# A pre-LayerNorm transformer block whose LayerNorm steps on VectorE change their form, with the planner's constants that go with them

## The chip, the cores and the metric

The kernel runs on one core of a Trainium2 chip. A core has five engines that run side by side [...]: TensorE (PE, matrix products), ScalarE (ACT, functions such as the exponential), VectorE (DVE), GpSimd (POOL), and SyncE (SP), which here issues nearly all DMAs. The metric is the device time of one execution in microseconds, the median of several runs.

## What is computed

One transformer block on 2048 rows of 640 in bf16: attention with 32 heads of 20 that share one key and one value head, then a gated MLP with 1536 hidden units, each behind a LayerNorm without weights and with a residual.

```python
def _layernorm(x, axis=-1, eps=1e-5):
    m = jnp.mean(x, axis=axis, keepdims=True)
    v = jnp.var(x, axis=axis, keepdims=True)
    return (x - m) / jnp.sqrt(v + eps)
...
q = (x @ wq).reshape(B, S, H, Dh).transpose(0, 2, 1, 3)
k = x @ wk
v = x @ wv
scores = jnp.einsum("bhqd,bkd->bhqk", q, k) * (Dh ** -0.5)
p = _softmax(scores, axis=-1)
o = jnp.einsum("bhqk,bkd->bhqd", p, v)      # heads joined, then @ wo
...
g = jnp.einsum("bsd,df->bsf", x, w_gate)
u = jnp.einsum("bsd,df->bsf", x, w_up)
return jnp.einsum("bsf,fd->bsd", _gelu(g) * u, w_down)
...
h = x + _A_ref(_layernorm(x), A_wq, A_wk, A_wv, A_wo)
h2 = h + _B_ref(_layernorm(h), B_w_gate, B_w_up, B_w_down)
```

## The kernel before

**Tiles and stages.** The rows are 16 tiles of 128. LN1 normalises each tile, and the result is transposed (tiles 0 and 1 on TensorE, the others by a DMA transpose) into xn1T. From it come the keys kT4, the values v_ext and the queries. The queries are worked in nine chunks of 2, 2, 2, 2, 2, 2, 2, 1 and 1 tiles, and a chunk is split into units of 512 columns, 32 units in all. For each unit and each of the 16 key tiles one *pack* of four score blocks (128 keys x 512 columns, one PSUM bank each) is computed; that is 512 packs and 2048 blocks. When a unit's weighted sums are complete, they are copied to osb, transposed by DMA to onr, divided by the softmax sum into onq (normed, L681), and when a chunk is complete its onq tiles are transposed by DMA to onT (L762), multiplied by wo and added to x. Then LN2 follows on those tiles, their DMA transpose to xn2T, and the MLP of the chunk, which runs beside the attention of the next chunk. The last tile's MLP comes alone at the end.

**Two ways to an exponential.** ScalarE takes blocks one or two at a time (L1519). VectorE can take a block too (L1620): it writes a 16-bit integer to pd slot 0 whose bits, read as bf16, approximate the exponential. Two shifted copies of it in pd slots 1 and 2 refine it; they come from integer adds, usually both in one GpSimd instruction (add_both, L1586), or one of the two on VectorE (do_adds, L1562) and the other alone on GpSimd (L1568). All three copies enter the weighted sum, so such a block costs TensorE three products in place of one. There are eight pd slots.

**The order.** Nothing is decided on the chip. When the program is built, a planner (_Plan) simulates the five engines with a fixed cost and a latency for each operation, and at each moment a greedy rule for an engine picks what it issues next (pe_decide, act_decide, dve_decide, pool_decide, sp_decide). The lists that result are emitted with semaphore waits, and each engine executes its list strictly in order. A cost that is changed therefore changes the whole order after it, and an operation that takes longer than planned stalls its engine's list.

Rules that matter here:
- issue_qk (L1120) decides how many of a pack's four blocks VectorE takes. One is usual. Two are taken when VectorE's expected load (dve_load, L1085) is under 450 ns, few adds are pending, and the comparison of ScalarE's expected stalls leaves more than SP2G (L1135, below). In dve_load each pending half add counts ADDW/2 and each block that waits ADDW on top of its 600.
- dve_decide (L1596) considers an add on VectorE only when at least PADD_LEN adds are pending.
- The norm of a tile (L513) is a task with lock set (L509): dve_decide holds it back while GpSimd's list reaches more than LOCKW = 200 ns ahead (L1653), commit (L80) places it after the GpSimd operation that runs at its start and GpSimd's next operation after it, and pool_decide (L1687) issues nothing while such a norm is due within YIELD = 500 ns. The VectorE adds are committed with lock as well.
- A DMA transpose costs SP 1330 ns and is taken as visible 1700 ns later for LN1 and LN2, 1500 ns later for onr and onT.

```python
            stall(t, 1, fb) + 1382.0 - stall(t, 2, fb) - 956.0 > SP2G[ph]):
```

**LayerNorm.** ln_half (L434) makes bn_stats of each half row and bn_aggr, giving mean and variance in mv. ln_group (L446) then takes the one or two tiles of a group together: the variances are copied to bf16 (L455, ln_vb), EPS is added (L459, ln_veb), GpSimd takes the square root as a power of 0.5 (L463, ln_denb), and VectorE the reciprocal (L467, ln_r). Then each tile is normalised by one tensor_scalar with two per-partition scalars (L513). LN1 has nine groups at the start, LN2 nine over the run.

Of the kernel before, what the change touches and what calls it, by code (L numbers as in the profile page):

```python
# [4 lines left out]
ALU = mybir.AluOpType  # L5
BF16 = mybir.dt.bfloat16
# [3 lines left out]
P = 128  # L10
# [7 lines left out]
CH_W = (1.0, 0.79296875, 0.63671875)  # L18
# [201 lines left out]
def bass_sequential_preLN__grouped_kv_mqa__glu_gated_geglu__prompt_kernel(  # L220
# [87 lines left out]
    xn_tmp = sb("xn_tmp", [P, NXT, D], BF16)  # L308
    stats = sb("stats", [P, 2, NT, 12], F32)
    mv = sb("mv", [P, 2, NT, 2], F32)  # L310
    ln_vb = sb("ln_vb", [P, 2, NT], BF16)
    ln_veb = sb("ln_veb", [P, 2, NT], BF16)
    ln_denb = sb("ln_denb", [P, 2, NT], BF16)
    ln_r = sb("ln_r", [P, 2, NT], F32)
    wq_stage = gbuf[:].rearrange("p f n -> p (f n)")[:, 0:NC_D * D].rearrange("p (c n) -> p c n", c=NC_D)
    pd16 = pd[:].bitcast(BF16)
# [34 lines left out]
    SP2 = 1  # L351
    SP2D = (450.0, 450.0, 450.0)
    SP2P = (3, 3, 3)
    SP2G = (300.0, 300.0, 300.0)
    ADD_MIN = 1
    PVF = 99
    QUIET = 0.55
    FTODO = 4
    PADD_DVE = 1
    PADD_LEN = (3, 3, 3)  # L360
    PRA = 3
    PRD = 3
    TH0 = 1500.0
# [8 lines left out]
    YIELD = 500.0  # L372
    WQA = 1
    W_LAT = 3000.0
    ADDW = 100.0
    MISCMAX = 1500.0
    L_PE, L_ACT, L_DVE, L_POOL = 232.0, 310.0, 150.0, 100.0

# [1 line left out]
    def load(eng, o, i, key, lat, after=()):  # L380
        return plan.commit(eng, (lambda e: e.dma_start(o, i)), 480.0, lat, reads=after, writes=key, dma=True)

    load("sp", xh[:, 0, :], x_view[:, 0, :], [("x", 0)], 2000)
    load("act", wk_sb[:], cview(A_wk), ["wk"], 2500)
    load("sp", xh[:, 1, :], x_view[:, 1, :], [("x", 1)], 2300)
    load("act", wq_stage[:, :, 0:HALF], cview(A_wq)[:, :, 0:HALF], [("wqs", 0)], 4500)
# [9 lines left out]
    def pool(fn, cost, reads=(), writes=()):  # L396
# [4 lines left out]
    pool(lambda e: e.affine_select(out=ident[:], in_=ident[:], compare_op=ALU.not_equal, fill=1.0, base=0,  # L401
                                   pattern=[[-1, P]], channel_multiplier=1), 450, ["ident0"], ["ident"])
    pool(lambda e: e.memset(halfc[:], 0.5), 40, writes=["halfc"])
    pool(lambda e: e.memset(wk4[:].bitcast(F32), 0.0), 300, writes=["wk4z"])
    pool(lambda e: e.memset(wq_pad[:, 0:4, :, :].bitcast(F32), 0.0), 1150, writes=[("wqz", 0)])
    plan.commit("dve", lambda e: e.memset(wq_pad[:, 4:8, :, :].bitcast(F32), 0.0), 1400, L_DVE,
# [39 lines left out]
    def ln_group(ln, tiles, prio, done):  # L446
        n = len(tiles)
        sl = slice(tiles[0], tiles[-1] + 1)
        cnt = [0]
        kk = (ln, tiles[0])  # L450

        def after_stats(op):
            cnt[0] += 1
            if cnt[0] == n:
                dve(lambda e: e.tensor_copy(ln_vb[:, ln, sl], mv[:, ln, sl, 1]), 80,  # L455
                    [("mv", ln, t) for t in tiles], [("vb", kk)], prio, c2)

        def c2(op):
            dve(lambda e: e.tensor_scalar_add(ln_veb[:, ln, sl], ln_vb[:, ln, sl], EPS), 80,  # L459
                [("vb", kk)], [("veb", kk)], prio, c3)  # L460

        def c3(op):
            task(("pool",), lambda e: e.tensor_tensor(ln_denb[:, ln, sl], ln_veb[:, ln, sl], halfc[:, 0:n], ALU.pow),  # L463
                 780, L_POOL, [("veb", kk), "halfc"], [("den", kk)], prio, c4)

        def c4(op):
            dve(lambda e: e.reciprocal(ln_r[:, ln, sl], ln_denb[:, ln, sl]), 90, [("den", kk)], [("lr", kk)],  # L467
                prio, c5)

        def c5(op):  # L470
            for t in tiles:
                norm(t)

        def norm(t):
            slot = []

            def gate():
                return bool(slots["xt"])

            def start():  # L480
                slot.append(slots["xt"].pop(0))
                return slot[0]

            def then(op):
                s = slot[0]

                def tdone(op2):
                    slots["xt"].append(s)
                    done(t, op2)

                if ln == 0:
                    o = xn1T[:, :, t * P:(t + 1) * P]
                    wkeys = [("xn1T", t)]
                else:
                    o = xn2T[:, :, xcol[t]:xcol[t] + P]
                    wkeys = [("xn2T", xcol[t])]
                def free():
                    return ln == 0 or all(up_left[x] == 0 for x in xshare[batch_of[t]])

                if t in (PE_T1 if ln == 0 else PE_T2):  # L500
                    tr_job(("tr", ln, t), xn_tmp[:, s, :], ("xt", s), o, wkeys, lambda: slots["xt"].append(s),
                           lambda op2: done(t, op2))
                    return
                sp_tasks.append(_Task(("sp",), lambda e: e.dma_start_transpose(o, xn_tmp[:, s, :]), 1330, 1700,
                                      [("xt", s)], wkeys, prio, tdone, free))

            keys = [("x", t)] if ln == 0 else [("h", t, 0), ("h", t, 1)]
            tk = _Task(("dve",), None, 320, L_DVE, keys + [("lr", kk)], [], prio, then, gate)
            tk.lock = True  # L509

            def bind():
                s = start()
                tk.fn = lambda e: e.tensor_scalar(xn_tmp[:, s, :], xh[:, t, :], mv[:, ln, t, 0:1],  # L513
                                                  ln_r[:, ln, t:t + 1], ALU.subtract, ALU.mult)
                tk.writes = [("xt", s)]

            tk.born = bind
            tasks.append(tk)

        return after_stats  # L520
# [68 lines left out]
    def kv_job(tiles):  # L589
        n = len(tiles) * P  # L590
        t0 = tiles[0]
        pieces = []
        for c in range(NC_D):
            pieces.append((mm(lambda b: bank(b, n), wk4[:, c, :], xn1T[:, c, t0 * P:t0 * P + n],
                              c == 0, c == NC_D - 1), c_mm(n), [("xn1T", t) for t in tiles] + ["wk4k", "wk4v"]))

        def then(b):
            def kfin(op):
                for t in tiles:
                    key_ready[t] = op  # L600
# [12 lines left out]

        def vthen(b):
            nt = len(tiles)
            vi = ps[:, b * 512:b * 512 + 32 * nt].rearrange("p (t e) -> p t e", t=nt)[:, :, 0:Dh]

            def vfin(op):
                free_bank(b)
                for w in (1, 2):  # L620
                    task(("pool",), (lambda w: lambda e: e.tensor_scalar(
                        v_ext[:, t0:t0 + nt, w, 0:Dh], v_ext[:, t0:t0 + nt, 0, 0:Dh], CH_W[w], None, ALU.mult))(w),
                        180 + 75 * nt, L_POOL, [("v", t, 0) for t in tiles] + [("vone", w)],
                        [("v", t, w) for t in tiles], 0)
# [96 lines left out]
    def on_job(u, so):  # L721
        if u["id"] in PE_ON:
            pieces = []
            for j in range(4):
                pieces.append((mm((lambda j: lambda b: ps[:, b * 512 + j * P:b * 512 + (j + 1) * P])(j),
                                  osb[:, so, j * P:(j + 1) * P], ident[:], True, True), c_mm(128),
                               [("osb", so), "ident"]))

            def then(b):
                slots["osb"].append(so)  # L730
                normed(u, so, bank(b), ("b", b), lambda: free_bank(b))
            jobs.append(_Job(("on", u["id"]), 1.5, pieces, then,
                             lambda: all(x in on_sent for t in u["tiles"] for x in on_before[t])))
            return
        tk = _Task(("sp",), None, 1330, 1500, [("osb", so)], [], 0.5, None, lambda: bool(slots["onr"]))
        sl = []

        def bind():
            s = slots["onr"].pop(0)
            sl.append(s)  # L740
            tk.writes = [("onr", s)]
            tk.fn = lambda e: e.dma_start_transpose(onr[:, s, :].rearrange("p (j i) -> p j i", j=4), osb[:, so, :])

        def sent(op):
            s = sl[0]
# [15 lines left out]

    def on_transpose(t):  # L762
        sl = []
        tk = _Task(("sp",), None, 1330, 1500, [("onq", onslot[t], g) for g in range(NG)], [], 1.0, None,
                   lambda: bool(slots["onT"]))

        def bind():
# [1071 lines left out]
```

The softmax here doesn't subtract the row's maximum and nothing guards it: scores larger than these inputs give would overflow.

## Time and profile before

| quantity | us |
|---|---|
| median of 6 runs (lowest to highest) | 787.71 (786.75 to 790.07) |
| the profiled execution's own time | 789.03 |
| its span, first to last instruction | 787.2 |
| ScalarE exponentials, 413 of two blocks and 598 of one | 437.8 + 363.3 |
| VectorE exponentials, 624 | 417.5 |
| GpSimd double adds, 577 | 588.1 |
| GpSimd single adds, 47 | 31.5 |
| VectorE adds, 25 | 15.4 |

In the profile, busy is the time in which an engine has at least one instruction under way; the sum of the durations of a group can be more, since two neighbours on one engine overlap. The mean duration of a group includes what an instruction waits after it has started. "Idle before" is the time in which the engine had nothing and what released it. The lines of a helper stand for every operation that it issues, so L565 is every piece of projection or MLP on TensorE. The last attention pack's exponentials end at 760.9 us; what follows is the last tile's output projection, LN2 and MLP, one after the other.

### The profile page before, as it was taken

How to read it: one execution, taken by the hardware profiler on the slowest of the kernel's cores; microseconds unless marked ns; L12 is line 12 of the kernel's file. 1: busy time of each engine (PE TensorE's matmuls, PEld its weight loads, DVE VectorE, ACT ScalarE, POOL GpSimd, SP SyncE). 2: the span in 40 equal slices, each digit the busy share in tenths (PEclk: the TensorE clock that was granted, in tenths of full speed). 3: DMA queues.
4: the chain of work that ended last, by engine and by line, in shares of the span. 5: the costliest groups of instructions: out<-in, count | busy, mean ns of one | idle time of the engine just before them, and what ended most of it. 6: DMA issues, size and time to landing. Idle time of an engine off the chain costs nothing.

```text
span 787.2 us, 29885 instructions
## 1 busy us (share of the span) xinstructions
PE 702.0 (89%) x13140; PEld 332.9 (42%) x13140; DVE 610.5 (78%) x1096; ACT 730.1 (93%) x1058; POOL 660.9 (84%) x713
## 2 busy tenths in 40 slices
PE   4698888888889998999888899899998999989998
PEld 3332233432335454444234444445543444434467
DVE  7768878778888777877787777777779787878854
ACT  5799999999999998999999999999999999999981
POOL 5489998989989898888998989789888898889760
PEclk9999999999999999999999999999999999999999
DMA  6554401000110002100010002200021000111000
GB/s 195 85 126 139 119 8 25 19 10 8 25 26 9 2 26 27 26 26 8 9 26 19 9 10 43 26 26 3 10 42 26 9 2 18 35 25 18 11 20 18
DMA packets 56769, 25.90 MB, mean 33 GB/s; under 512 B 47808, under 2 KB 55360, under 8 KB 56640
## 3 DMA queue, kind: packets, MB, share of 16 engines
q1 hardware_dynamic: 55328, 23.55, 13.9%
q8 instruction: 105, 1.72, 1.0%
q10 hardware_dynamic: 1312, 0.44, 0.2%
q14 instruction: 24, 0.20, 0.1%
HBM read 10.21 MB, written 2.62 MB: 16 GB/s over the span
## 4 chain that ended last, share of the span: by engine, by line
PE 53%; ACT 23%; DVE 17%; DMA 4%; issue 2%; POOL 1%
PE ps L565 20%; ACT pa L1519 19%; PE ps L1256 15%; PE ps L1177 15%; DVE pd L1620 9%; PE ps L561 3%; ACT gbuf L905 3%; DVE xn_tmp L513 1%; DVE osb L1283 1%; DMA onT<-onq 1%; DMA onr<-osb 1%; DVE stats L443 1%; PE ps L1382 1%; DMA xh<-in_A_x_dram 1%; ACT L1519 1%
## 5 line engine op out<-in xcount | busy, mean ns | idle before, releaser
L1519 ACT ACTIVATE pa<-ps 128x512 bf16<-128x512 f32 (+1 forms) x1011 | 684.6, 814 | 27.8 <-PE ps L1177 22.6
L1586 POOL TENSOR_TENSOR pd<-pd,shifts 128x512 int32<-128x512 int32 x577 | 588.1, 1039 | 75.8 <-DVE pd L1620 70.8
L1620 DVE TENSOR_SCALAR pd<-ps 128x512 uint16<-128x512 f32 x624 | 417.5, 687 | 139.6 <-PE ps L1177 131.0
L1256 PE MATMUL ps<-pd,v_ext 128*32 128x512 bf16 x1872 | 285.3, 384 | 18.3 <-DVE osb L1283 11.9
L1256 PE MATMUL ps<-pa,v_ext 128*32 128x512 bf16 x1424 | 256.8, 384 | 4.4 <-ACT pa L1519 2.0
L1177 PE MATMUL ps<-qT,kT 32*128 32x512 bf16 x2048 | 203.0, 385 | 40.7 <-DVE pd L1620 22.9
L1177 PEld LDWEIGHTS ps<-qT,kT 32*128 32x128 bf16 x2048 | 56.1, 91 | 205.7 <-DVE pd L1620 127.2
L1256 PEld LDWEIGHTS ps<-pd,v_ext 128*32 128x32 bf16 x1872 | 78.1, 95 | 79.1 <-issue 32.3
L1256 PEld LDWEIGHTS ps<-pa,v_ext 128*32 128x32 bf16 x1424 | 69.9, 95 | 42.9 <-issue 22.3
L565 PE MATMUL ps<-xn2T,wg_sb 128*32 128x256 bf16 (+1 forms) x1736 | 68.0, 272 | 1.4 <-DMA xn2T<-xn_tmp 0.7
L565 PE MATMUL ps<-xn2T,wu_sb 128*32 128x256 bf16 x1680 | 67.2, 274 | 1.9 <-DVE gbuf L922 1.5
L565 PE MATMUL ps<-wd_sb,gbuf 128*32 128x320 bf16 x1344 | 66.3, 301 | 0.0
L565 PE MATMUL ps<-xn1T,wq_pad 128*32 128x256 bf16 (+1 forms) x1440 | 51.5, 267 | 0.8 <-POOL wq_pad L988 0.6
L565 PEld LDWEIGHTS ps<-xn2T,wu_sb 128*32 128x32 bf16 x1680 | 42.9, 96 | 20.9 <-issue 9.5
L565 PEld LDWEIGHTS ps<-xn2T,wg_sb 128*32 128x32 bf16 x1736 | 43.0, 96 | 20.1 <-issue 11.9
L565 PEld LDWEIGHTS ps<-wd_sb,gbuf 128*32 128x32 bf16 x1344 | 34.3, 96 | 24.0 <-issue 11.6
L922 DVE TENSOR_TENSOR gbuf<-ps,gbuf 128x512 bf16<-128x512 f32 x48 | 32.7, 681 | 9.7 <-PE ps L561 6.4
L565 PEld LDWEIGHTS ps<-xn1T,wq_pad 128*32 128x32 bf16 x1440 | 33.5, 98 | 15.5 <-issue 7.5
L1382 PE MATMUL ps<-kT,zz 128*32 128x512 bf16 x428 | 39.4, 394 | 0.0
L443 DVE BATCH_NORM_STATS2 stats<-xh 128x6 f32<-128x320 bf16 x64 | 29.8, 474 | 2.2 <-DMA xh<-in_A_x_dram 1.9
L1568 POOL TENSOR_TENSOR pd<-pd,shifts 128x256 int32<-128x256 int32 x47 | 31.5, 687 | 0.0
L565 PE MATMUL ps<-wo_sb,onT 128*32 128x320 bf16 x600 | 28.9, 301 | 2.8 <-DMA onT<-onq 2.6
(73 smaller groups left out, 348.2 us busy)
## 6 DMA issues: line engine op xcount, KB each, us to landing
out_dram<-xh SPq DMA_DIRECT2D x16, 160.0 KB, 1.8
xh<-in_A_x_dram SPq DMA_DIRECT2D x3, 640.0 KB, 7.3
wd_sb<-in_B_w_down_dram SPq DMA_DIRECT2D x4, 480.0 KB, 3.7
wg_sb<-in_B_w_gate_dram SPq DMA_DIRECT2D x3, 384.0 KB, 3.2
wu_sb<-in_B_w_up_dram SPq DMA_DIRECT2D x3, 384.0 KB, 3.1
wg_sb<-in_B_w_gate_dram SPq DMA_DIRECT2D x1, 768.0 KB, 4.2
wu_sb<-in_B_w_up_dram SPq DMA_DIRECT2D x1, 768.0 KB, 4.5
wo_sb<-in_A_wo_dram SPq DMA_DIRECT2D x1, 480.0 KB, 3.6
```

Of the source, the lines that this page charges most:

```text
L443: dve(lambda e: e.bn_stats(stats[:, ln, t, 6 * h:6 * h + 6], xh[:, t, h * HALF:(h + 1) * HALF]), 395, [key], [("st", ln, t, h)], prio, c)
L561: return e.matmul(o(b), l, r, start=st, stop=sp)
L565: ins = e.matmul(o(b)[a, :], l[:, a], r, start=st, stop=sp, tile_position=(0, 32 * j))
L905: task(("act",), (lambda v: lambda e: e.activation(v, v, ACT.Gelu_apprx_tanh))(v), ("gelu", c_act(n * (f1 - f0))), L_ACT, ks, ks, 1.0, (la ...
L922: dve(lambda e: e.tensor_tensor(o, i, o, ALU.mult), c_dve(n * k), [("b", bk)] + ks, ks, 1.0, fin)
L1177: ins = e.matmul(bank(b), kT4[32 * r:32 * r + 32, kt * P:(kt + 1) * P], qT[32 * r:32 * r + 32, s, :], start=True, stop=True, tile_position ...
L1256: ins = e.matmul(ps[32 * r:32 * r + 32, ab * 512:(ab + 1) * 512], v_ext[:, it["kt"], it["w"], :], it["ap"], start=st, stop=(j in ends), ti ...
L1382: ins = e.matmul(ps[32 * r:32 * r + 32, ab * 512:ab * 512 + n * P], zz[:], kT4[:, 0:n * P], start=False, stop=False, tile_position=(0, 32 ...
L1519: op = plan.commit("act", lambda e: e.activation(dst, src, ACT.Exp, scale=SM_SCALE), cost, L_ACT, [("b", b0 + i) for i in range(n)], [("pa ...
L1568: return e.tensor_tensor(pd32[:, w, h], pd32[:, 0, h], shifts[:, w - 1:w].to_broadcast([P, 256 * k]), ALU.add)
L1586: return e.tensor_tensor(pd32[:, 1:3, h], pd32[:, 0, h].unsqueeze(1).to_broadcast([P, 2, 256 * k]), shifts[:].unsqueeze(2).to_broadcast([P ...
L1620: op = plan.commit("dve", lambda e: e.tensor_scalar(pd[:, 0, s * 512:(s + 1) * 512], bank(b), CH_A, CH_B, ALU.mult, ALU.add), c_dve(512), ...
```

## The change

The two small steps before the square root become tensor_reduce sums over the innermost axis: the first sums one element (a copy of the variance to bf16, into column 0 of a ln_vb that now has two columns), the second sums two, the variance and EPS, which a new GpSimd memset has put into column 1. The norm's output is written as five rows of 128 in place of one run of 640, at the same addresses; its planned cost is 420 in place of 320, and it has no lock any more, so that LOCKW and YIELD no longer act on it. DMA transposes are planned to be visible T_LAT later: 1700 for LN1 as before, 2700 for LN2, onr and onT. The load of the first tile is planned with 2750 in place of 2000, the power with 690 in place of 780. SP2G goes from 300 to 200, PADD_LEN from 3 to 4, ADDW from 100 to 60. The GpSimd scaling of v_ext gets a second operator that adds 0.

```diff
-    ln_vb = sb("ln_vb", [P, 2, NT], BF16)
-    ln_veb = sb("ln_veb", [P, 2, NT], BF16)
-    ln_denb = sb("ln_denb", [P, 2, NT], BF16)
+    ln_vb = sb("ln_vb", [P, 2, NT, 2], BF16)
+    ln_ve = sb("ln_ve", [P, 2, NT], BF16)
+    ln_den = sb("ln_den", [P, 2, NT], BF16)
...
-    SP2G = (300.0, 300.0, 300.0)
+    SP2G = (200.0, 200.0, 200.0)
...
-    PADD_LEN = (3, 3, 3)
+    PADD_LEN = (4, 4, 4)
...
-    ADDW = 100.0
+    T_LAT = (1700.0, 2700.0, 2700.0)
+    ADDW = 60.0
...
-    load("sp", xh[:, 0, :], x_view[:, 0, :], [("x", 0)], 2000)
+    load("sp", xh[:, 0, :], x_view[:, 0, :], [("x", 0)], 2750)
...
+    pool(lambda e: e.memset(ln_vb[:, :, :, 1:2], EPS), 60, writes=["eps"])
...
-                dve(lambda e: e.tensor_copy(ln_vb[:, ln, sl], mv[:, ln, sl, 1]), 80,
-                    [("mv", ln, t) for t in tiles], [("vb", kk)], prio, c2)
+                narrow(ln_vb[:, ln, sl, 0], mv[:, ln, sl, 1:2], [("mv", ln, t) for t in tiles], [("vb", kk)], c2)
+
+        def narrow(o, i, reads, writes, then):
+
+            def fn(e):
+                with nc.allow_low_precision("one or two terms, rounded once"):
+                    return e.tensor_reduce(o, i, mybir.AxisListType.X, ALU.add)
+            dve(fn, 80, reads, writes, prio, then)

         def c2(op):
-            dve(lambda e: e.tensor_scalar_add(ln_veb[:, ln, sl], ln_vb[:, ln, sl], EPS), 80,
-                [("vb", kk)], [("veb", kk)], prio, c3)
+            narrow(ln_ve[:, ln, sl], ln_vb[:, ln, sl, :], [("vb", kk), "eps"], [("ve", kk)], c3)

         def c3(op):
-            task(("pool",), lambda e: e.tensor_tensor(ln_denb[:, ln, sl], ln_veb[:, ln, sl], halfc[:, 0:n], ALU.pow),
-                 780, L_POOL, [("veb", kk), "halfc"], [("den", kk)], prio, c4)
+            task(("pool",), lambda e: e.tensor_tensor(ln_den[:, ln, sl], ln_ve[:, ln, sl], halfc[:, 0:n], ALU.pow),
+                 690, L_POOL, [("ve", kk), "halfc"], [("den", kk)], prio, c4)
...
-                sp_tasks.append(_Task(("sp",), lambda e: e.dma_start_transpose(o, xn_tmp[:, s, :]), 1330, 1700,
+                sp_tasks.append(_Task(("sp",), lambda e: e.dma_start_transpose(o, xn_tmp[:, s, :]), 1330, T_LAT[ln],
                                       [("xt", s)], wkeys, prio, tdone, free))
...
-            tk = _Task(("dve",), None, 320, L_DVE, keys + [("lr", kk)], [], prio, then, gate)
-            tk.lock = True
+            tk = _Task(("dve",), None, 420, L_DVE, keys + [("lr", kk)], [], prio, then, gate)
...
-                tk.fn = lambda e: e.tensor_scalar(xn_tmp[:, s, :], xh[:, t, :], mv[:, ln, t, 0:1],
+
+                tk.fn = lambda e: e.tensor_scalar(xn_tmp[:, s, :].rearrange("p (a b) -> p a b", a=5), xh[:, t, :], mv[:, ln, t, 0:1],
                                                   ln_r[:, ln, t:t + 1], ALU.subtract, ALU.mult)
...
-                        v_ext[:, t0:t0 + nt, w, 0:Dh], v_ext[:, t0:t0 + nt, 0, 0:Dh], CH_W[w], None, ALU.mult))(w),
+                        v_ext[:, t0:t0 + nt, w, 0:Dh], v_ext[:, t0:t0 + nt, 0, 0:Dh], CH_W[w], 0.0, ALU.mult, ALU.add))(w),
...
-        tk = _Task(("sp",), None, 1330, 1500, [("osb", so)], [], 0.5, None, lambda: bool(slots["onr"]))
+        tk = _Task(("sp",), None, 1330, T_LAT[2], [("osb", so)], [], 0.5, None, lambda: bool(slots["onr"]))
...
-        tk = _Task(("sp",), None, 1330, 1500, [("onq", onslot[t], g) for g in range(NG)], [], 1.0, None,
+        tk = _Task(("sp",), None, 1330, T_LAT[2], [("onq", onslot[t], g) for g in range(NG)], [], 1.0, None,
                    lambda: bool(slots["onT"]))
```

More of the change, by code (lines that the diff above doesn't have):

```diff
@@ L454, in after_stats @@
             if cnt[0] == n:
-                dve(lambda e: e.tensor_copy(ln_vb[:, ln, sl], mv[:, ln, sl, 1]), 80,
-                    [("mv", ln, t) for t in tiles], [("vb", kk)], prio, c2)
+                narrow(ln_vb[:, ln, sl, 0], mv[:, ln, sl, 1:2], [("mv", ln, t) for t in tiles], [("vb", kk)], c2)
[4 more added lines that the diff above has]
+            dve(fn, 80, reads, writes, prio, then)
         def c2(op):
-            dve(lambda e: e.tensor_scalar_add(ln_veb[:, ln, sl], ln_vb[:, ln, sl], EPS), 80,
-                [("vb", kk)], [("veb", kk)], prio, c3)
+            narrow(ln_ve[:, ln, sl], ln_vb[:, ln, sl, :], [("vb", kk), "eps"], [("ve", kk)], c3)
         def c3(op):
-            task(("pool",), lambda e: e.tensor_tensor(ln_denb[:, ln, sl], ln_veb[:, ln, sl], halfc[:, 0:n], ALU.pow),
-                 780, L_POOL, [("veb", kk), "halfc"], [("den", kk)], prio, c4)
+            task(("pool",), lambda e: e.tensor_tensor(ln_den[:, ln, sl], ln_ve[:, ln, sl], halfc[:, 0:n], ALU.pow),
+                 690, L_POOL, [("ve", kk), "halfc"], [("den", kk)], prio, c4)
         def c4(op):
-            dve(lambda e: e.reciprocal(ln_r[:, ln, sl], ln_denb[:, ln, sl]), 90, [("den", kk)], [("lr", kk)],
+            dve(lambda e: e.reciprocal(ln_r[:, ln, sl], ln_den[:, ln, sl]), 90, [("den", kk)], [("lr", kk)],
                 prio, c5)
```

## The prediction

> **What bounds the kernel now.** I read the page's busy shares first, then the busy time in stretches of 20 us.
>
> ```profile
> PE 702.0 (89%) x13140; PEld 332.9 (42%) x13140; DVE 610.5 (78%) x1096; ACT 730.1 (93%) x1058; POOL 660.9 (84%) x713
> ```
>
> The stretches (columns: stretch, its length, then busy us and instruction count of PE, PEld, DVE, ACT and POOL, clock, DMA share, GB/s):
>
> ```profile
> 100.00:120.00 20.00, 16.76 (x239) 5.93 (x235) 15.94 (x27) 19.79 (x32) 19.72 (x23) 1.00 0.04 8
> ...
> 300.00:320.00 20.00, 17.74 (x352) 8.39 (x344) 15.40 (x28) 18.46 (x28) 15.74 (x17) 1.00 0.24 25
> ...
> 460.00:480.00 20.00, 20.00 (x411) 9.52 (x403) 14.74 (x25) 19.49 (x30) 18.46 (x19) 1.00 0.12 24
> ...
> 600.00:620.00 20.00, 17.05 (x393) 8.48 (x396) 16.90 (x30) 18.71 (x28) 17.70 (x19) 1.00 0.13 25
> ```
>
> ScalarE is the limit: over 60 to 760 us the same view sums to 678.4 us of ACT in 700, so 21.6 us are idle. POOL is close behind it where attention runs alone (19.72 of 20), TensorE where the MLP runs too (20.00). VectorE always has room, but only on average. The chain of waits gives PE 53% and ACT 23%: it changes engine all the time, which fits a machine where ACT, PE and POOL hand over in one fixed order.
>
> So there are three sources of gain: the 21.6 us of ACT gaps, ACT's own work, and the ends (0 to 60, 760 to 787).
>
> Where do the LayerNorm steps stand? From the groups with shapes kept apart (count, then busy us, mean ns, idle before):
>
> ```profile
> L513 DVE TENSOR_SCALAR xn_tmp<-xh,mv,ln_r 128x640 bf16<-128x640 bf16 x32 | 17.7, 570 | 0.1
> L1562 DVE TENSOR_SCALAR pd<-pd 128x1024 uint16<-128x1024 uint16 x20 | 12.5, 626 | 0.0
> L455 DVE CAST ln_vb<-mv 128x2 bf16<-128x2 f32 x14 | 5.5, 391 | 0.1
> L459 DVE TENSOR_SCALAR ln_veb<-ln_vb 128x2 bf16<-128x2 bf16 x14 | 3.9, 279 | 0.1
> ...
> L455 DVE CAST ln_vb<-mv 128x1 bf16<-128x1 f32 x4 | 0.6, 150 | 0.1
> ```
>
> A two-element cast has a mean of 391 ns where the one-element cast takes 150. The timeline of one group shows why:
>
> ```profile
> 219.30 1.04 POOL L1586 TENSOR_TENSOR pd<-pd,shifts 128x512 int32<-128x512 int32 x1 [0.22 <-DVE ln_vb L455]
> 219.34 1.03 DVE L459 TENSOR_SCALAR ln_veb<-ln_vb 128x2 bf16<-128x2 bf16 x1
> ```
>
> The tiny VectorE operation starts 0.04 us after a Pool add and ends at 220.37, when that add (to 220.34) is done. It was held, not computing. Other members of the two groups take 0.15 to 0.17 us.
>
> The last places are the transposes, in the chain of waits in order of time (start, us, what):
>
> ```profile
> 138.94 4.21 DMA xn2T<-xn_tmp
> ...
> 303.78 4.45 DMA onT<-onq
> ...
> 582.27 4.50 DMA onT<-onq
> ```
>
> [...] The trace of before holds no tensor_reduce and no five-row output, so neither is shown yet.
>
> **The change part by part.**
>
> *Holds removed.* Excess over an unheld instance: L455 14 x (391-160) = 3.2 us, L459 14 x (279-150) = 1.8, L513 32 x (570-440) = 4.2 (440 is the line's median; alone, at 771.8 us, it takes 0.45). Together 9.2 us of VectorE, about 8 of them in the eight groups after 130 us. That is not yet time. Stretches around those groups (131-141, 217-229, 320-332, 405-417, 498-510, 599-611, 687-699, 734-742, 90 us in all) have ACT busy for 84.7, so 5.3 us of ACT gaps lie there. Bounds 0 to 5.3; I take 3, because each held operation stands ahead of an exponential on VectorE that frees a score bank, but the groups also bring their own extra work.
>
> *The norm itself.* [...] Sixteen in the head, sixteen later. Later: [...] on an engine with room. In the head VectorE is the limit for a while (9.97 of 10 us between 20 and 30), and LayerNorm feeds the first keys: [...] I take +1.5. In the tail one norm lies in the serial end: +0.2. The tensor_reduce forms: nearest row 150 ns, two elements, bounds -0.05 to +0.1 us each, hidden; 0. The EPS memset, which the second of them now waits for (nearest row, a small memset, 0.10 us), lies in Pool's early wait, done long before the first variance at 5.0 us. The v_ext scaling with a second operator: nearest row 341 ns, 18 of them, 0.
>
> *No lock in the order.* The norm no longer makes the order keep Pool idle for it (YIELD) or hold the norm until Pool is free (LOCKW). At 606.9 us Pool had been idle 0.86 us beside a norm, at 225.3 us 1.22. About 1 us in each of eight groups: 8 us of Pool that the order can fill with eight more adds of 1.04 us.
>
> *More exponentials off ACT.* A score pack has four blocks. In the planner's prices a pack with one block on VectorE costs ACT 1382 ns and with two 956. The trace fits: 13 instructions in 8.69 us are 0.668 each, against 1382/2. VectorE has 624 blocks of 512 packs now, so at least 112 packs give it two. SP2G 300 to 200 lets two be chosen at 100 ns more stall, ADDW 100 to 60 makes the pending adds count less. Each further pack saves ACT 0.43 us and costs Pool 1.04. Pool's recovered 8 us pay for about 8 packs, its slack in the MLP stretches for some more, and PADD_LEN 4 takes capacity away. Bounds -10 to +30 packs, +4 to -13 us; I take 10 packs, -4 us.
>
> *Slack for transposes.* The order now expects a transpose visible 2.83 us after issue (1330+1500) for onr and onT, 3.03 for xn2T; after, 4.03. The second of a pair really lands after 4.2 to 4.5. ACT gaps stand exactly there: 1.44 us in 300-310, 1.78 in 580-590, 1.17 in 140-150, together 4.4. 4.03 covers most of the lateness, and PE gets other work placed ahead. No queue is moved past another; every LN1 transpose keeps 1700. Bounds +1 (later chains, with no cover) to -4.4; I take -3.5. The x0 load's 2750 says what happens now (first statistics at 3.35 us): 0.
>
> Sum: -3 + 1.5 + 0.2 - 4 - 3.5 = -8.8 us. The profiled execution took 789.03 (span 787.2 and 1.8 around it), giving 780.2. It stands 1.3 above the median of the runs, so on the median 787.71 - 8.8 = 778.9, call it 779.
>
> **The rivals.**
>
> *A, Pool becomes the bound (slower).* Today 25 VectorE adds (L1562) relieve Pool of one half of 47 blocks, 17 of them before 235 us, where Pool is at 93 to 99% in most stretches of 20 us. With PADD_LEN 4 those start later or not at all: each block back on Pool costs 1.039 - 0.687 = 0.35 us, up to 16.5 us in all; SP2G adds more blocks to the same queue. With pd slots held longer, VectorE can't start the next exponential, score banks stay taken and ACT starves. If 60% of 16.5 lands where Pool is full (+10) and the holds and slack give back 5: 787.7 + 5 = 793. For it: 19.72 of 20. Against: the order still moves adds to VectorE once four wait, and Pool gains 8 us. It decides from the point where Pool stays above 98% while ACT falls below 95%.
>
> *B, all hidden.* ACT is busy 97% between 60 and 760; if its order closes the gaps by itself only the head's +1.5 and some of the slack count: 787. For it: VectorE, whose holds go, has 22% idle.
>
> *C, the form doesn't do it.* If rows that touch are taken as one run, the norm keeps its 0.44 us [...], now without a reserved place: up to 1 us of hold on each of 16, perhaps 0.6 as a mean, 10 us of VectorE, half of it in ACT: 790.
>
> *D, the shift is large.* 30 packs: -13 in place of -4: 770.
>
> **How the numbers follow.** Forecast 0.46, A 0.22, B 0.12, C 0.07, D 0.13. What this kernel's measurement can tell from no change is about 0.2%, 1.6 us. Faster: forecast and D, and a fifth of B, 0.61; same: most of B, 0.09; slower: A, C and a rest of B, 0.30. The forecast's own range is 773 to 785; 80% reaches from D to A, 769 to 795.
>
> **What would show it.** Right: [...] no small LayerNorm operation near 1 us; more than 624 exponentials on VectorE, ACT's total lower; PE without 1 us waits on onT; ACT gaps from 60 to 760 us well under 21.6. Wrong: L513 still at 0.44 with outliers (C); L1562 nearly gone with Pool full and ACT gaps grown (A); the same ACT total and the same gaps (B).

## The result, and the profile after

The changed kernel takes 785.13 us (median of 16 runs, 783.02 to 787.12); the kernel before took 788.37 in the runs beside it. The ratio is 0.9958, interval 0.9948 to 0.9969: 3.3 us faster, where 8.8 were forecast. The two profiled executions lie further apart than that, 789.03 and 783.95 us (spans 787.2 and 782.1), because the one before is above its median and the one after below. Differences of 1 or 2 us in time between these two traces are therefore not taken as effects of the change; the timed ratios carry the prices.

The busy shares of the page after:

```profile
PE 704.6 (90%) x13039; PEld 335.0 (43%) x13039; DVE 598.0 (76%) x1071; ACT 729.1 (93%) x1058; POOL 668.6 (85%) x710
```

ScalarE has 1.0 us less to do than before (730.1), VectorE 12.5 us less, Pool 7.7 more. The same stretches of 20 us as before, and one more, 380 to 400 (columns as before: stretch, length, busy us and count of PE, PEld, DVE, ACT and POOL, clock, DMA share, GB/s):

```profile
100.00:120.00 20.00, 16.41 (x199) 5.27 (x202) 12.77 (x20) 18.62 (x29) 19.80 (x21) 0.91 0.04 7
...
300.00:320.00 20.00, 18.74 (x390) 9.34 (x386) 18.04 (x35) 19.90 (x29) 16.03 (x17) 1.00 0.21 26
...
380.00:400.00 20.00, 15.78 (x197) 4.91 (x189) 16.10 (x23) 16.75 (x27) 17.77 (x21) 0.91 0.13 25
...
460.00:480.00 20.00, 19.33 (x388) 9.25 (x380) 14.45 (x25) 19.66 (x30) 17.23 (x18) 1.00 0.06 19
...
600.00:620.00 20.00, 17.41 (x358) 8.41 (x346) 15.85 (x26) 19.51 (x30) 17.97 (x20) 1.00 0.20 25
```

In the stretches where transposes had been late, ACT is fuller: 19.90 against 18.46 in 300 to 320, 19.51 against 18.71 in 600 to 620. The work in a stretch is not quite the same in both, since the order differs. In the stretch 380 to 400 ACT loses 3.25 us; it is looked at with the experiments below.

The groups on VectorE, shapes kept apart (count, then busy us, mean ns, idle before):

```profile
L1627 DVE TENSOR_SCALAR pd<-ps 128x512 uint16<-128x512 f32 x621 | 415.4, 687 | 142.7 <-PE ps L1184 134.2
...
L520 DVE TENSOR_SCALAR xn_tmp<-xh,mv,ln_r 128x640 bf16<-128x640 bf16 x32 | 19.1, 616 | 0.3
...
L1569 DVE TENSOR_SCALAR pd<-pd 128x1536 uint16<-128x1536 uint16 x2 | 3.8, 1887 | 0.0
...
L463 DVE TENSOR_REDUCE ln_ve<-ln_vb 128x2 bf16<-128x4 bf16 x14 | 2.1, 148 | 0.2
...
L463 DVE TENSOR_REDUCE ln_vb<-mv 128x2 bf16<-128x2 f32 x14 | 2.0, 146 | 0.0
```

Three things are to be seen. The two small steps, which in the change share the helper's line L463, went from means of 391 and 279 ns to 146 and 148. The norm kept its form: its mean is 616 ns (570 before), and its list of instructions shows the old pattern:

```profile
L520 DVE TENSOR_SCALAR xn_tmp<-xh,mv,ln_r x32: 391/442/1224, 6.2 to 763.5; 128x640 bf16<-128x640 bf16 x32
```

These are the minimum, median and maximum in ns: 0.44 us, and up to 1.22 where it is held. The norm at 318.01 us shows such a hold: it starts 0.03 us after a Pool add of 1.04 us and takes 1.19; the last, at 763.47, with Pool idle, takes 0.45. And the exponentials on VectorE are 621, three fewer than before, while the additions of 1024 elements (20 before) have gone; two of 1536 are left.

The timeline of the LayerNorm group that was shown of before, now with the sum over an axis:

```profile
224.42 1.04 POOL L1593 TENSOR_TENSOR pd<-pd,shifts 128x512 int32<-128x512 int32 x1 [0.75 <-DVE ln_vb L463]
224.44 0.16 DVE L463 TENSOR_REDUCE ln_ve<-ln_vb 128x2 bf16<-128x4 bf16 x1
```

It starts 0.02 us after a Pool add, as before, and takes 0.16 us instead of 1.03. The chain of waits after has these DMA steps and no other:

```profile
0.72 2.50 DMA xh<-in_A_x_dram
3.23 3.89 DMA xh<-in_A_x_dram
19.32 4.18 DMA xn1T<-xn_tmp
```

The transposes of onT, onr and xn2T that stood in it (3.92 to 4.65 us each) are gone.

Last, ScalarE between 60 us and the end of its last exponential, and the rest of the span, first before and then after:

```profile
60.00:760.90 700.90, 637.33 (x12035) 293.20 (x12035) 556.48 (x943) 679.33 (x987) 621.08 (x642) 1.00 0.12 25
760.90:787.20 26.30, 23.52 (x363) 20.30 (x360) 10.35 (x22) 6.26 (x9) 2.02 (x3) 1.00 0.04 15
```

```profile
60.00:753.60 693.60, 637.35 (x11927) 293.38 (x11920) 540.02 (x911) 677.79 (x983) 629.13 (x637) 1.00 0.12 24
753.60:782.10 28.50, 25.66 (x337) 21.78 (x335) 11.26 (x24) 6.27 (x9) 0.72 (x2) 1.00 0.07 25
```

Attention ends 7.3 us earlier: ACT's idle time there falls from 700.9 - 679.3 = 21.6 to 693.6 - 677.8 = 15.8 us, and it has 1.5 us less to do. The part after it is 2.2 us longer, so some of the gain is given back at the end. These two figures, the idle time up to the last exponential and the length of the end, are used for the experiments as well.

### The profile page after: what moved, and what is told of

It reads as the page before. It is cut to its first block, busy times and chain, and to the rows that moved or that the text cites. A ratio compares the mean times of both kernels' runs of the same rounds, so it can differ in the third digit from the quotient of the medians.

```text
span 782.1 us, 29651 instructions
## 1 busy us (share of the span) xinstructions
PE 704.6 (90%) x13039; PEld 335.0 (43%) x13039; DVE 598.0 (76%) x1071; ACT 729.1 (93%) x1058; POOL 668.6 (85%) x710
## 4 chain that ended last, share of the span: by engine, by line
PE 59%; ACT 21%; DVE 14%; POOL 3%; issue 2%; DMA 1%; DVEq 0%
PE ps L572 21%; ACT pa L1526 17%; PE ps L1263 17%; PE ps L1184 16%; DVE pd L1627 8%; PE ps L568 3%; POOL pd L1593 3%; ACT gbuf L912 2%; DVE xn_tmp L520 1%; PE ps L1389 1%; DVE osb L1290 1%; DMA xh<-in_A_x_dram 1%; ACT L1526 1%; ACT L912 1%; DVE stats L445 1%
## 5 line engine op out<-in xcount | busy, mean ns | idle before, releaser
L1526 ACT ACTIVATE pa<-ps 128x1024 bf16<-128x1024 f32 (+1 forms) x1011 | 684.1, 830 | 22.1 <-PE ps L1184 15.4
L1593 POOL TENSOR_TENSOR pd<-pd,shifts 128x512 int32<-128x512 int32 x615 | 623.9, 1039 | 66.6 <-DVE pd L1627 60.2
L1263 PE MATMUL ps<-pd,v_ext 128*32 128x512 bf16 x1863 | 291.4, 385 | 16.1 <-DVE osb L1290 7.8
L1263 PEld LDWEIGHTS ps<-pd,v_ext 128*32 128x32 bf16 x1863 | 81.8, 95 | 75.6 <-issue 30.5
L572 PE MATMUL ps<-xn2T,wg_sb 128*32 128x256 bf16 x1680 | 66.3, 274 | 0.4 <-DVE gbuf L885 0.3
L572 PE MATMUL ps<-xn2T,wu_sb 128*32 128x256 bf16 x1680 | 64.3, 274 | 1.2 <-DVE gbuf L929 1.0
L572 PE MATMUL ps<-wd_sb,gbuf 128*32 128x320 bf16 x1268 | 61.0, 301 | 0.1
L572 PE MATMUL ps<-wo_sb,onT 128*32 128x320 bf16 x600 | 31.1, 302 | 0.8 <-DVE xh L807 0.6
L885 DVE CAST gbuf<-ps 128x512 bf16<-128x512 f32 x42 | 28.7, 684 | 0.5 <-PE ps L572 0.2
```

The lines of the kernel that those rows point to most:

```text
L572: ins = e.matmul(o(b)[a, :], l[:, a], r, start=st, stop=sp, tile_position=(0, 32 * j))
L885: dve(lambda e: e.tensor_copy(o, i), c_dve(n * k), [("b", bk)], ks, 1.0, fin)
L1263: ins = e.matmul(ps[32 * r:32 * r + 32, ab * 512:(ab + 1) * 512], v_ext[:, it["kt"], it["w"], :], it["ap"], start=st, stop=(j in ends), ti ...
L1526: op = plan.commit("act", lambda e: e.activation(dst, src, ACT.Exp, scale=SM_SCALE), cost, L_ACT, [("b", b0 + i) for i in range(n)], [("pa ...
L1593: return e.tensor_tensor(pd32[:, 1:3, h], pd32[:, 0, h].unsqueeze(1).to_broadcast([P, 2, 256 * k]), shifts[:].unsqueeze(2).to_broadcast([P ...
```

## The experiments

The order of the whole kernel is computed from planned prices, so nearly every edit also gives a new order of some thousand instructions. Experiments that keep the order exactly are marked as such; they are the firm ones. (The traces of these pairs list the same instructions in the same sequence on ScalarE, VectorE and GpSimd, but for the edited ones.) All ratios are to the kernel before, timed beside each run, with a 95% interval. "After" stands for the changed kernel.

### The forms of the small steps (e1, e2; orders kept)

e1 is the kernel before, its order unchanged, with only this edit (and the memset of EPS):

```
-    dve(lambda e: e.tensor_copy(ln_vb[:, ln, sl], mv[:, ln, sl, 1]), ...)
+    narrow(ln_vb[:, ln, sl, 0], mv[:, ln, sl, 1:2], ...)
-    dve(lambda e: e.tensor_scalar_add(ln_veb[:, ln, sl], ln_vb[:, ln, sl], EPS), ...)
+    narrow(ln_veb[:, ln, sl], ln_vb[:, ln, sl, :], ...)
```

> The kernel before with the two small LayerNorm steps as tensor_reduce and nothing else; every engine's list keeps its order. Theory 1 (the holds of the small steps are the gain): the steps go from means of 391 and 279 ns to about 150, 5.0 us of VectorE less, and the time falls by 2 to 4 us (ratio 0.995 to 0.9975). Theory 2 (the slack for transposes is the gain): under 1 us (above 0.9985). Theory 3 (the gain is a draw of the new order): under 1 us too.

e2 is the reverse: after, its order unchanged, with the cast and the addition of EPS back.

> The changed kernel in exactly its order, with the cast and the tensor_scalar of before in place of the two sums. Theory 1: the small steps are held again for about 5 us of VectorE and 2 to 4 us of the gain are lost (ratio to before 0.998 to 1.001). Theories 2 and 3: within 1 us of the changed kernel (ratio 0.9945 to 0.997).

Measured: e1 785.96 us, ratio 0.9975 (0.9963 to 0.9987). e2 786.19 us, 0.9988 (0.9978 to 0.9998), where after has 0.9958. So the forms bring 2.0 us in before's order (by the interval 1.0 to 2.9) and 0.9988 - 0.9958, 2.4 us, in after's, with about 1.2 us to either side. The groups of e2:

```profile
L468 DVE TENSOR_SCALAR ln_ve<-ln_vb 128x2 bf16<-128x2 bf16 x14 | 6.0, 430 | 0.2
L457 DVE CAST ln_vb<-mv 128x2 bf16<-128x2 f32 x14 | 4.7, 333 | 0.0
```

and its timeline at the place shown above, the same two instructions in the same order:

```profile
225.12 1.04 POOL L1595 TENSOR_TENSOR pd<-pd,shifts 128x512 int32<-128x512 int32 x1 [0.76 <-DVE ln_vb L457]
225.16 1.03 DVE L468 TENSOR_SCALAR ln_ve<-ln_vb 128x2 bf16<-128x2 bf16 x1
```

Only the form differs between 1.03 and 0.16 us. All small steps together are 11.9 us of VectorE in e2 and 5.3 in after: 6.6 us of VectorE, nearly all of it held time, are worth 2.4 us of the kernel.

Could the granted clock of TensorE make this gain instead? It differs a little from run to run, and among the runs of one kernel those with 0.001 more are 0.4 to 0.55 us faster (a line through the runs of before, e1, e2 and e4). The mean is 0.9946 in e1 and 0.9937 in before beside it, so 0.4 of the 2.0 us may be the clock's. But after, at 0.992, is faster than e2 at 0.993. So the clock doesn't make the gain.

### The slack for transposes (e4, e5, e6)

e4 is the kernel before with the new slack alone; e5 is after with the old slack; e6 is after with the new slack in all but the last two chunks (chunks count from 0).

```
e4:  -  1330, 1700, (LN2)    -  1330, 1500, (onr, onT)
     +  1330, 2700           +  1330, 2700
e5:  -  T_LAT = (1700.0, 2700.0, 2700.0)
     +  T_LAT = (1700.0, 1700.0, 1500.0)
e6:  +  T_LAT[...] if chunk < 7 else 1700.0 (LN2), 1500.0 (onr, onT)
```

> The kernel before with only the transposes of LN2, onr and onT planned 2700 ns late. Theory 2: PE's waits on onT and xn2T of over 1 us go, the ScalarE gaps near 140-150, 300-310 and 580-590 close and the time falls by 3 to 4.4 us (0.9945 to 0.996), perhaps less what the tail takes back. Theory 1: nothing beyond the draw of a new order, within 1.5 us.

> The changed kernel with the transposes planned as before (visible 1700 ns later for LN2, 1500 for onr and onT), all else changed. If the slack is a real part of the gain: PE waits on onT of 1 us or more come back, ScalarE idles over 20 us between 60 us and the last exponential (15.8 in the changed kernel), the last exponential ends 4 to 7 us later and the tail is back near 26.4 us: 1.5 to 4 us slower than the changed kernel (ratio to before 0.998 to 1.001). If the gain of the slack was a draw of the order, anything from 0.988 to 1.004.

> The changed kernel with the slack for all but the two last chunks, so that the order differs only near the end (some 205 of 2758 rows on TensorE). If the slack delays the last MLP past the end of attention: the tail of 28.5 us falls to about 26.5 and the time by 1 to 2 us (ratio to before 0.993 to 0.995). If the longer tail only follows from attention ending earlier: the same as the changed kernel within 0.8 us.

Measured: e4 785.25 us, 0.9974 (0.9964 to 0.9985), 2.0 us faster than before. e5 792.42 us, 1.0070 (1.0047 to 1.0092), 1.1% slower than after. e6 785.11 us, 0.9962 (0.9947 to 0.9976), the same as after.

The waits of VectorE in e5 show a transpose that is waited for again:

```profile
DVE rcp L703 <- DMA onr<-osb: 7.4, 8, 1.5
```

(us in all, times, longest). On onT TensorE's products wait 0.3 us in e5 and its weight loads 1.1, at most 0.6 at once, so the single waits of 1 us that were expected there did not come back. After has no wait on onr, onT or xn2T at all; before had 2.1 us on onr and on onT 2.6 (products) and 2.0 (weight loads). e4 has 0.2 on onr and 0.2 on onT. ACT's idle time to the last exponential is 23.9 us in e5 against 15.8. In e4 it is 16.4:

```profile
60.00:754.40 694.40, 638.35 (x12009) 292.42 (x12005) 560.35 (x949) 678.00 (x987) 621.22 (x640) 1.00 0.12 25
754.40:783.90 29.50, 26.72 (x362) 22.60 (x360) 11.54 (x25) 5.54 (x8) 2.01 (x3) 1.00 0.07 24
```

Attention ends 6.5 us earlier than before, and the end is 3.2 us longer. What is left at the last exponential shows where: the products of the down projection that stand behind it take 11.2 us in e4 (90 of them, 24 on a quarter of the array), 7.0 in before (48) and 9.8 in after (67). So TensorE had left more MLP work for the end. e6 was meant to shorten the end by taking the slack away there. It did not: 11.2 us of such products and an end of 29.7 us. The slack in the last two chunks is not what lengthens the end.

### A form that does what the norm was meant to do (e7, e8; same order)

The access pattern that the trace keeps with each instruction is the same for the norm before and after: an output of one run of 640 elements. The five rows of 128 touch, and in the compiled instruction they are merged. To test rows that don't touch, they must lie at a pitch, and a DMA transpose that reads them there was not tried. So e7 moves all LN2 transposes to TensorE, and e8 is e7, its order unchanged, with rows of 128 at a pitch of 132 for LN2, which the transposes read there too.

```
e7:  -  PE_T2 = (15,)
     +  PE_T2 = tuple(range(16))
e8:  -  xn_tmp = sb("xn_tmp", [P, NXT, D], BF16)
     +  xn_tmp = sb("xn_tmp", [P, NXT, 660], BF16)
     -  ...tensor_scalar(xn_tmp[:, s, :].rearrange("p (a b) -> p a b", a=5), ...
     +  ...tensor_scalar(xn_tmp[:, s, 0:D] if ln == 0 else xn_tmp[:, s, :].rearrange("p (a b) -> p a b", a=5)[:, :, 0:P], ...
```

> The changed kernel with LN2's transposes on TensorE instead of by DMA; only a ground for the next run. Its norms should still be at 0.44 us when Pool is idle and up to 1.2 us beside a Pool add, since five rows that touch are one run of 640 in the instruction. The time can be anything within 1% of the changed kernel, as the order is a new one.

> The run before in exactly its order, with LN2's norms written to five rows of 128 at a pitch of 132, so that they can't be taken as one run. [...] none near 1 us, and if held norms cost time, the kernel is 0.5 to 2 us faster than the run before (ratio of the two 0.9975 to 0.9995). If the pitch changes nothing on the engine: 0.44 us with outliers and the same time. [...]

Measured: e7 790.73 us, 1.0044 (1.0028 to 1.0060). e8 787.68 us, 1.0006 (0.9995 to 1.0017): 3.05 us less than e7. The sixteen LN2 norms of e7 (minimum, median and maximum ns):

```profile
L520 DVE TENSOR_SCALAR xn_tmp<-xh,mv,ln_r x16: 416/718/1253, 141.4 to 773.1; 128x640 bf16<-128x640 bf16 x16
```

and of e8:

```profile
L520 DVE TENSOR_SCALAR xn_tmp<-xh,mv,ln_r x16: 524/596/606, 141.3 to 768.9; 128x640 bf16<-128x640 bf16 x16
```

The shape column is the same, the time is not. e7 writes its five rows touching, as after does, in whose trace they are one run of 640; e8 writes them at a pitch of 132. There the median norm takes 0.60 us and none of the sixteen more than 0.61. Over the sixteen, the mean falls from 0.79 to 0.59 us, 3.2 us of VectorE in all. What part the transposes have, which read the rows at the pitch in e8, was not shown. So in this order the form without holds goes with a gain of about 3 us, although its 0.60 us is more than the 0.45 of a norm beside an idle Pool. The change asked for this and did not get it. e7 is 0.9% slower than after, with a new order in it, so e8 is no improvement of the whole.

### The balance and the lock (e10, e11, e13)

```
e10: -  _Task(("dve",), None, 420, ...)      e11: -  PADD_LEN = (4, 4, 4)
     +  _Task(("dve",), None, 320, ...)           +  PADD_LEN = (3, 3, 3)
     +  tk.lock = True
e13: e11, and   -  SP2G = (200.0, ...), ADDW = 60.0
                +  SP2G = (300.0, ...), ADDW = 100.0
```

> The kernel after with the norm planned as before: the order again keeps Pool clear of it (lock, 320 ns). The norm on the chip is the same in both, 0.44 us [...]. Theory 1 (losing the lock costs something [...]): the line's mean goes from 616 ns back to about 570, 1.5 us of VectorE in all, and the time falls by up to 1 us, ratio 0.994 to 0.996. Theory 2 (the lock itself, in which the order leaves Pool idle, was the cost): slower by about 1 to 3 us, 0.998. A new order alone moved the time by up to 1% in e3, so only a move together with the norm's mean counts for theory 1.

> The kernel after with PADD_LEN 3 in place of 4, so that VectorE takes over adds of 1024 elements once three wait, some 30 times in place of 2. Theory 1 (4 was a loss: a 1536 add waited 3.1 us for Pool and Pool is full in more stretches): Pool's busy share falls by about 1.5 points, no VectorE add above 2.2 us, and the time falls by 2 to 3 us, ratio 0.993. Theory 2 (25 adds fewer on VectorE make room for the exponentials that ACT waits for): slower by 2 to 3 us, 0.999. Theory 3 (neither counts beside the new order): anywhere within 1%, and no relation to Pool's share.

> The kernel after with all three numbers of the balance as before: SP2G 300, ADDW 100, PADD_LEN 3. Against e11, which undoes PADD_LEN alone, only SP2G and ADDW differ; the order puts 629 exponentials on VectorE against e11's 633. Theory 1 (the two numbers move next to no exponential, so my term of 4 us was nothing): the time of e11 within 1 us, ratio 0.993 to 0.996, and ACT's busy total within 1.5 us of e11's 725.5. Theory 2 (they do help ACT, by another way than the count): slower than e11 by 2 to 4 us, 0.997 to 0.999.

Measured: e10 785.01 us, 0.9971 (0.9960 to 0.9982); the norm's held pattern stays (mean 624 ns, median 446, maximum 1275), so the lock in the order didn't protect it, and theory 1 falls; that the lock costs time is not settled either, with 1 us against after and intervals that overlap. The kernels of before's side show the same: e4 has the lock, and its norms have a mean of 619 ns.

```profile
L513 DVE TENSOR_SCALAR xn_tmp<-xh,mv,ln_r 128x640 bf16<-128x640 bf16 x32 | 19.3, 619 | 0.1
```

e11 782.64 us, 0.9944 (0.9927 to 0.9960). e13 784.92 us, 0.9967 (0.9957 to 0.9976). e11 is some 1.1 us faster than after, as theory 1 has the sign, but only half of its size and with overlapping intervals; its Pool share fell from 668.6 to 662.8 us, 0.6 points of the span instead of 1.5; its 27 additions of 1024 elements took 708 ns as a mean, and the longest was not shown. e13 came out between its two theories, 1.8 us slower than e11, with ACT's total 727.2 us against 725.5. The exponentials on VectorE in e11 and in e13:

```profile
L1627 DVE TENSOR_SCALAR pd<-ps 128x512 uint16<-128x512 f32 x633 | 422.8, 687 | 127.0 <-PE ps L1184 115.9
```

```profile
L1627 DVE TENSOR_SCALAR pd<-ps 128x512 uint16<-128x512 f32 x629 | 420.8, 688 | 134.1 <-PE ps L1184 123.9
```

So the new SP2G and ADDW come with four exponentials more on VectorE and 1.7 us less of ACT (e13 to e11), and PADD_LEN 4 in place of 3 with twelve fewer and 3.6 us more of ACT (e11 to after). Each is a pair of two orders. The six kernels with all three numbers as in after (after, e5, e6, e7, e10, e12) have 621 to 628, by their orders and what else differs in them, so a step of 4 may be no more than that; 633 lies outside.

What the long additions cost can be seen at one place of after, in the stretch 380 to 400 from above:

```profile
390.81 1.75 POOL L1575 TENSOR_TENSOR pd<-pd,shifts 128x256 int32<-128x256 int32 x3
390.88 3.09 DVE L1569 TENSOR_SCALAR pd<-pd 128x1536 uint16<-128x1536 uint16 x1
...
392.52 1.04 POOL L1593 TENSOR_TENSOR pd<-pd,shifts 128x512 int32<-128x512 int32 x1
...
394.12 0.39 PE L1263 MATMUL ps<-pd,v_ext 128*32 128x512 bf16 x2 [2.38 <-DVE pd L1569]
...
395.39 1.15 ACT L1526 ACTIVATE pa<-ps 128x512 bf16<-128x512 f32 x2 [2.19 <-PE ps L1184]
```

VectorE's addition starts 0.07 us after Pool's first half add and ends 0.41 us after the fourth Pool instruction (392.52 + 1.04 = 393.56). The other such addition of after took 0.68 us. PE waits 2.38 us for the long one, ACT 2.19 us for PE. After this stall the clock column, which gave 0.91 for the stretch, falls to half for some 4 us:

```profile
394.00:396.00 2.00, 1.68 (x15) 0.56 (x17) 1.19 (x3) 0.61 (x2) 1.04 (x1) 0.63 0.00 0
396.00:398.00 2.00, 2.00 (x21) 0.52 (x20) 1.34 (x3) 1.20 (x3) 1.84 (x2) 0.51 0.04 8
```

A score product takes 0.60 us there (median 603 ns of eight) in place of 0.38 (384 ns from 388 to 392 us), and ACT waits for PE again, 0.80 us at 397.33. So not all of the 3.25 us is the wait itself. Such a phase needs no long addition: after has one at 114 to 118 us (0.66 and 0.50), before one at 692 to 696 (0.65 and 0.50). What starts it is not shown. All this is one place of one trace; before had no addition above 1.09 us.

### How much of a difference is only a new order (e3, e12, e14)

Three kernels in which one planned number changes and no instruction does. The loads, the power and all operands stay; only the order is another.

```
e3  (before):  x0 load planned at 2000 -> 2750 ns
e12 (after):   Pool's power planned at 690 -> 780 ns
e14 (before):  Pool's power planned at 780 -> 690 ns
```

> The kernel before with only the planned latency of the first load at 2750 in place of 2000, an edit that gives the chip nothing, but a new order everywhere. Theories 1 and 2: within 0.15% of before (0.9985 to 1.0015). Theory 3 (a new order alone moves the time): off by 0.2% or more, either way; this measures the size of such a draw.

> The kernel after with one planned number as before: 780 ns in place of 690 for Pool's power of the LayerNorm step. On the chip that step stays what it is, 0.69 us; only the order changes, in some two thirds of the TensorE rows. Theory 1 (a new order by itself is worth up to 1%, e3): a time that differs from the kernel after by 1 us or more in either direction, with the same 146 ns small steps and the same 0.44 us norm. Theory 2 (e3 was an exception and orders are alike): within 0.15% of after, 0.9958.

> The kernel before with one planned number of the change: 690 ns in place of 780 for Pool's power of the LayerNorm step, which takes 0.69 us on the chip in both. Nothing but the order changes, in nearly half of the TensorE rows. Theory 1 (a new order is a draw and before's own is an ordinary one): within 1% of 1 to either side, as likely slower as faster; a difference of over 1.5 us would be a second case like e3. Theory 2 (e3 was slow because of what it did, telling the order that the first load comes later while nothing else was changed, and orders are otherwise alike, as e12 has it): within 0.2% of 1.

Measured: e3 795.2 us, 1.0087 (1.0061 to 1.0113). e12 784.16 us, 0.9962 (0.9945 to 0.9979), as after. e14 790.25 us, 1.0037 (1.0024 to 1.0051). Both numbers are part of the change. e3's stretch to the last exponential:

```profile
60.00:769.30 709.30, 641.76 (x12158) 296.16 (x12154) 563.76 (x949) 679.73 (x990) 627.99 (x649) 1.00 0.12 24
```

ACT is idle for 29.6 us, 8 more than in before, with the same work. So a new order alone moved this kernel by 0 to 7 us. Each experiment above that does not keep its order carries that doubt, and so does the change as a whole.

### The two parts that pay, without the rest (e9; the order of e4)

e9 is the kernel before with e1's forms and e4's slack: no five rows, the lock kept, the balance as before.

> The kernel before with the sums over an axis for the two small steps (as in e1) and with 2700 ns of slack for the transposes of LN2, onr and onT (as in e4); the order is exactly e4's. Theory 1 (forms and slack each work by themselves and add): against e4 a further gain of about 2 us, e1's 0.9975 times e4's 0.9974, ratio 0.995, some 784.4 on e4's scale, i.e. as fast as the whole change or faster. Theory 2 (e4's longer tail, not the small steps, sets its end): 0.997 as e4.

Measured: 782.32 us, 0.9942 (0.9925 to 0.9959). Against e4, whose order it has, that is 0.9942 / 0.9974, 2.5 us: the forms are worth 2.0, 2.4 and 2.5 us in three orders. The last of these is the least firm: e9 and e4 were timed apart, and the clock was higher in e9 (0.9965, and 0.9946 in before beside it, against 0.9941 and 0.9937), which by the line above is some 0.7 of the 2.5 us, an estimate. e9 is at least as fast as the whole change; their intervals overlap a little.

```profile
60.00:750.30 690.30, 635.39 (x11985) 292.56 (x11981) 556.65 (x946) 675.90 (x983) 619.22 (x639) 1.00 0.12 25
750.30:779.90 29.60, 26.78 (x363) 22.60 (x360) 11.54 (x25) 5.58 (x9) 2.06 (x3) 1.00 0.07 24
```

ACT's idle time falls further, to 14.4 us, and the end keeps e4's length.

## Why the prediction was right in sign and wrong in size

The sum was -3 + 1.5 + 0.2 - 4 - 3.5 = -8.8. What the runs put in its place is about -2.4 for the small steps and -2 for the slack, together -4.4; e9, which has these two alone, has -4.6. The change as a whole has -3.3. So the rest of it (balance, lock, prices) is left with about +1, as a remainder and not by a measurement of its own. The first term is firm, since it comes from fixed orders; the second and the remainder are single draws of the order. For such a draw the sum had no term at all: the new price of the x0 load stood at 0, and alone, in before, it gave 6.9 us (e3).

**Exponentials moved off ACT, -4: the term that failed.** I took ten more packs with two blocks on VectorE. There are 621 such exponentials instead of 624, and ACT's total fell by 1.0 us, not 4. Two premises fell with it. Pool did not win 8 us from the lock: with the lock back (e10) it is busy 667.7 us against 668.6. Its 7.7 us more than before come with the additions that VectorE no longer does, 2 instead of 25. And SP2G and ADDW brought four exponentials at most (e13 to e11), where I took ten packs, while PADD_LEN 4, for which I wrote only that it "takes capacity away", goes with twelve fewer (e11 to after). How much of these counts is the order's own scatter (621 to 628 with after's numbers) stays open.

**Slack for transposes, -3.5.** The mechanism was right: the waits on onr, onT and xn2T are gone in after, nearly gone in e4 (0.2 us on onr and on onT), and in e5 those on onr are back. The size was not: e4 gives -2.0, from one order. The working counted ACT's gaps (4.4 us) and took no account of the end. In its trace e4 won 6.5 us up to the last exponential and lost 3.2 after it, with more MLP work left behind. That e5 loses 1.1% fits the slack too, but is more than slack alone explains beside e4, and part of it may be the draw.

**Holds removed, -3.** For the small steps right, and rather too small: they held 5.0 of the 9.2 us I counted, and bring 2.0 to 2.5 us. That a sum would not be held was the author's estimate; before has no such sum. For the norm, the other 4.2 us, wrong, because its holds are still there. e8 is 3 us faster without them in e7's order, so the whole term, had it come, was probably nearer to the upper bound of 5.3. That -3 stands so near to -2.4 is therefore luck in part: one half was missing, and the other was worth more than its share.

**The norm itself, +1.5 in the head and +0.2 in the tail.** Both terms were the author's estimate; the trace of before has no norm in another form. The form was read from the view in the source. The instruction has one run of 640 in the trace of after, as in before, and keeps its 0.44 us (medians 442 and 440 ns). Where rows lie apart (e8) the norm takes 0.60 us and none is above 0.61. The head's loss didn't come: ACT is busy for 45.0 of the first 60 us, 44.5 before. The end grew by 2.2 us in the trace, and the products of the down projection in it by 2.8 us (9.8 against 7.0).

**The sum over an axis.** Right in both respects: 146 and 148 ns, within the bounds, and not one of the 36 above 0.16 us. Why none is held is not shown.

**The rivals.** C named what became of the norm exactly and gave it 0.07; its price was wrong. The norm's mean is 46 ns above before's, 1.5 us of VectorE over 32 of them, not 10, and even that isn't the missing lock: with the lock it is 624 ns (e10), 619 (e4) and 617 (e9). A was half there: the VectorE additions are nearly gone and Pool is full from 60 to 100 us (20.00 of 20 in both stretches), but ACT is full there as well (19.99 and 20.00), so the point from which A decides was not reached. Its cost is e11's 1 us, if that is no draw.

**The markers.** Of those named, small steps, waits on onT and ACT's gaps (15.8) came out as forecast; ACT's total fell by 1.0 us only, and the count of exponentials did not rise; the norm stayed at 0.44 us with outliers, the sign named for C.

What stays open: whether SP2G, ADDW and PADD_LEN cost anything by themselves. e11 and e13 differ from after by 1.1 and 0.7 us, and orders alone differ by more.

## What to carry to other kernels

The form of an instruction was here what was left after rows that touch had been merged; judge by its duration and spread in the trace (0.44 with holds to 1.22 in after, or 0.60 and none above 0.61 in e8), not by the view in the source. Small VectorE operations beside a busy Pool were worth rewriting here, as sums that were not held (146 and 148 ns in place of 391 and 279): all small steps, 6.6 us of VectorE in after's order, gave 2 to 2.5 us. And where an order is computed, measure a part with the order kept, or change a number that does nothing on the chip beside it: otherwise a draw of up to 0.9% is taken for an effect.

## What the runs showed of the hardware that was not expected

- A held VectorE instruction stayed behind several Pool instructions in a row, not behind one. The addition at 390.88 us in after starts 0.07 us after the first of four Pool instructions that follow each other without a gap, ends 0.41 us after the last and takes 3.09 us; the other addition of its size takes 0.68. In e2, with the same order, the longest took 3.11 us.
- The form of the norm that took 0.60 us, with a spread of 524 to 606 ns (e8), beat the one that takes 0.45 us beside an idle Pool but had a mean of 0.79 over the same sixteen (e7): 787.68 us against 790.73. Pool was busy for 85% of the span in after.
- TensorE's granted clock fell to about half for some 4 us at single places (0.63 and 0.51 at 394 to 398 us in after, 0.65 and 0.50 at 692 to 696 in before), and the median score product took 0.60 us there in place of 0.38. What starts such a phase is not shown.
